# Batch 0's chain with 4 zero products instead of 43, reordered slots, a fill on GpSimd, and the last two blocks as one more pair

## The chip, the cores and the metric

One NeuronCore of one Trainium2 chip. The metric is the device time of one execution in microseconds (us); every number of a run is the median of its fast executions unless said otherwise. A run is called slow when it is over 1.5% above the fastest of the same kernel. Engine names as the profile has them: PE is TensorE's products, PEld its weight loads, DVE VectorE, ACT ScalarE, POOL GpSimd, SP SyncE; a q behind the name is that engine's issue of transfers.

## The reference, cut to what matters

```python
# B = 8 batches, H = 8 heads, S = 576, D = 64, M = 32 memories, d_model = 512, d_ff = 1536
a = softmax over s of phi                 # bhsm
k_m, v_m = a.T @ k, a.T @ v               # bhmd
attn = softmax(q @ k_m.T / 8) @ v_m       # bhsd
x = attn as 4608 tokens x 512
out = ((x @ w_a) * (x @ w_b)) @ w_out     # float32 in and out
```

The kernel never builds `attn`. It multiplies the 32 memories of each head into `w_a` and `w_b` (a "fold", result `vab`), so that the up products are `A` (the normalised scores, 256 rows) times `vab`. The down products of two blocks of 128 tokens are done together with seven half-size products instead of eight (a "pair", with sums of tokens and of weights made ahead on GpSimd).

## The kernel before: the parts that the change touches

The program is written by units that are placed by hand into slots between the up products; the strings below are that schedule. `f3` is three zero products (they keep TensorE busy), `y3` three early down products, `ks`/`vs` the sums of k and v, `kt`/`vt` their transposes, `s`/`e`/`den`/`nr` scores, exp, denominators and the normalising product that gives `A`, `hv`/`v` a fold of 256 or 512 columns and `hx`/`x` its copy to SBUF. "Second weights" below means `w_b`; a transfer's "landing" is the time at which its data have arrived.

```python
    nc.vector.memset(kv_sbs[1][:, 2], 1.0 / CS)      # ones beside k and v of odd batches
    load_wab(256, 512)
    load_wab(512, 1024)
    load_wab(1024, 1536)
    load_wo(0); load_phi(1); load_k(1); load_q(1, halves[0]); load_wo(1); ...   # cut
    load_wo(2)

        def normalise(g, hfs=slice(0, 2)):
            ...                                       # R = exp(-L) on ScalarE
            engine = nc.vector if b < 3 else nc.gpsimd
            engine.tensor_tensor(out=attn[b][:, g, sl], in0=t["E"][:, g, sl], in1=t["R", g][:, sl], op=ALU.mult)

    def sum_weights():                                # four GpSimd sums of w_out's quarters
        ...
            nc.gpsimd.tensor_tensor(out=out, in0=in0, in1=in1, op=ALU.subtract)

    fill(16)
    chain(0, "exp0 exp1 ks0 f3 kt0 qt0 qt1 f14 s0 e0 ks1 f3 kt1 qt2 qt3 f6 den0 f4 s1 nr0 e1 f6 vs0 vs1 vt0 vt1 den1 f3 "
             "hv0a hx0a nr10 nr11 hv0b hx0b f4")
    ups(steps(0, 0, 4), slots(0, "- hv1a+hx1a - hv1b+hx1b - v1a+x1a - v1b+x1b"))
    load(2)
    ups(steps(0, 4, 12), slots(0, "- - - - v2a+x2a - v2b+x2b"))
    chain(1, "exp0 exp1 y9 ks0 y3 kt0 qt0 qt1 y1 ks1 y3 kt1 s0 e0 qt2 qt3 y6 den0 y2 s1 e1 nr0 y4 den1 y2 vs0 vs1 y1 vt0 vt1 nr1 y1 hv0a hx0a y2 hv0b hx0b y2")
    load(3)
    sum_weights()
    ups(steps(1, 0, 4), slots(1, "y1 hv1a+hx1a hv1b+hx1b y1 v1a+x1a v1b+x1b y3 y3"))
    ...                                               # batches 2 to 7, cut
    last_down(B // 2 * NI - 1)                        # last block: 12 + 12 products of 256 columns
```

The softmax here doesn't subtract the row's maximum and nothing guards it: scores larger than these inputs give would overflow.

## Time and profile before

| | before |
|---|---|
| time, 3 runs | 247.96 us (247.90 to 247.97) |
| span of the profiled run | 246.4 us |
| TensorE busy | 234.4 us (95%) |
| first up product | 20.45 us |
| last fold of batch 0's second weights | 31.45 us |
| batch 1's first early down product (its load) | 36.09 us |
| first single-half up step of batch 1 | 57.08 us |
| last up product done (first load of the rest) | 228.70 us |
| last weight load done | 241.86 us |
| last store's issue starts | 243.29 us |

The page's part 4, the chain that ended last by engine, says that transfers hold a sixth of it (all of them ahead of 48.4 us):

```profile
PE 74%; DMA 17%; DVE 3%; POOL 2%; ACT 1%; issue 1%; ACTq 0%; DVEq 0%; POOLq 0%
```

### The profile page before, as it was taken

How to read it: one execution, taken by the hardware profiler on the slowest of the kernel's cores; microseconds unless marked ns; L12 is line 12 of the kernel's file. 1: busy time of each engine (PE TensorE's matmuls, PEld its weight loads, DVE VectorE, ACT ScalarE, POOL GpSimd, SP SyncE). 2: the span in 40 equal slices, each digit the busy share in tenths (PEclk: the TensorE clock that was granted, in tenths of full speed). 3: DMA queues.
4: the chain of work that ended last, by engine and by line, in shares of the span. 5: the costliest groups of instructions: out<-in, count | busy, mean ns of one | idle time of the engine just before them, and what ended most of it. 6: DMA issues, size and time to landing. Idle time of an engine off the chain costs nothing.

```text
span 246.4 us, 7681 instructions
## 1 busy us (share of the span) xinstructions
PE 234.4 (95%) x3049; PEld 167.1 (68%) x3049; DVE 166.5 (68%) x401; ACT 157.9 (64%) x409; POOL 151.1 (61%) x123
## 2 busy tenths in 40 slices
PE   7589999999998999999999999999999999999993
PEld 3354574456655857777787777877787787888782
DVE  3636794477959967876994649865995686756620
ACT  2247772578697489578856768588855877565330
POOL 8724233499799029892899759892849186936000
PEclk9999999999999999999999999999999999999999
DMA  6999999999979804973159732695120303033145
GB/s 198 210 198 206 211 252 207 255 220 271 233 183 207 160 4 108 238 127 85 33 149 208 174 85 45 167 207 145 32 56 3 88 7 82 10 78 71 43 104 128
DMA packets 26036, 33.82 MB, mean 137 GB/s; under 512 B 1936, under 2 KB 20368, under 8 KB 26000
## 3 DMA queue, kind: packets, MB, share of 16 engines
q0 software_dynamic: 19280, 22.71, 50.3%
q1 hardware_dynamic: 6288, 9.90, 16.3%
q10 hardware_dynamic: 432, 0.72, 0.8%
q8 instruction: 24, 0.39, 0.6%
q14 instruction: 12, 0.10, 0.1%
HBM read 42.47 MB, written 9.44 MB: 211 GB/s over the span
## 4 chain that ended last, share of the span: by engine, by line
PE 74%; DMA 17%; DVE 3%; POOL 2%; ACT 1%; issue 1%; ACTq 0%; DVEq 0%; POOLq 0%
PE pa L602 18%; PE pb L612 16%; PE py L480 15%; PE pv L480 8%; DMA phi_sb<-in_phi_dram 6%; DMA wo_sb<-in_moe_w_out_dram 6%; DMA wb_sb<-in_moe_w_b_dram 5%; PE pva L337 5%; PE px L480 4%; PE po L389 3%; PE pkv L213 2%; PE pD L314 1%; PE pscore L292 1%; PE pT L242 1%; POOL q_sb L90 1%
## 5 line engine op out<-in xcount | busy, mean ns | idle before, releaser
L615 DVE TENSOR_TENSOR ht<-a_sb,pb 128x288 f16<-128x288 f16 x192 | 82.9, 448 | 40.2 <-ACT a_sb L605 29.3
L605 ACT CAST a_sb<-pa 128x288 f16<-128x288 f32 x192 | 74.7, 405 | 31.6 <-PE pa L602 31.0
L602 PE MATMUL pa<-A,vab 128*128 128x288 f16 x384 | 76.5, 287 | 1.4 <-DVE A L325 1.4
L612 PE MATMUL pb<-A,vab 128*128 128x288 f16 x384 | 76.5, 286 | 0.2
L463 POOL TENSOR_TENSOR h_sums<-ht 128x768 f16<-128x768 f16 x28 | 45.9, 1640 | 34.0 <-DVE ht L615 34.0
L612 PEld LDWEIGHTS <-vab 128*128 128x128 f16 x384 | 37.0, 98 | 13.2 <-issue 1.9
L602 PEld LDWEIGHTS <-vab 128*128 128x128 f16 x384 | 34.5, 98 | 15.9 <-issue 9.1
L480 PEld LDWEIGHTS <-h_sums 128*128 128x128 f16 x360 | 35.1, 98 | 6.5 <-issue 0.4
L349 ACT CAST vab<-pva 128x512 f16<-128x512 f32 (+1 forms) x52 | 28.1, 558 | 10.0 <-PE pva L337 10.0
L349 DVE CAST vab<-pva 128x512 f16<-128x512 f32 (+1 forms) x52 | 32.8, 643 | 2.4 <-PE pva L337 2.0
L480 PEld LDWEIGHTS <-ht 128*128 128x128 f16 x270 | 26.4, 98 | 5.4 <-issue 0.2
L480 PE MATMUL py<-w_sums,h_sums 128*128 128x256 f16 x180 | 28.5, 272 | 0.0
L463 POOL TENSOR_TENSOR h_sums<-h_sums,ht 128x768 f16<-128x768 f16 x14 | 23.1, 1650 | 1.0
L463 POOL TENSOR_TENSOR h_sums<-ht,h_sums 128x768 f16<-128x768 f16 x14 | 23.0, 1642 | 1.0
L305 ACT ACTIVATE E<-pscore 128x288 f16<-128x288 f32 x32 | 11.4, 416 | 13.6 <-PE pscore L292 13.5
L325 POOL TENSOR_TENSOR A<-E,R 128x576 f16<-128x576 f16 x10 | 12.8, 1278 | 11.9 <-ACT R L323 11.6
L389 PE MATMUL po<-wo_sb,ht 128*128 128x512 f16 x60 | 16.0, 381 | 0.1
L480 PE MATMUL py<-wo_sb,ht 128*128 128x256 f16 x90 | 15.2, 273 | 0.0
L480 PE MATMUL pv<-w_sums,h_sums 128*128 128x256 f16 x90 | 15.2, 273 | 0.0
L204 DVE STREAM_TRANSPOSE qT<-q_sb 128x288 f32<-128x288 f32 x32 | 14.5, 463 | 0.6 <-DMA q_sb<-in_q_dram 0.6
L480 PE MATMUL py<-w_sums,ht 128*128 128x256 f16 x90 | 14.7, 272 | 0.1
L315 ACT ACTIVATE L<-pD 128x288 f32<-128x288 f32 x32 | 11.4, 413 | 5.0 <-PE pD L314 4.8
(66 smaller groups left out, 273.1 us busy)
## 6 DMA issues: line engine op xcount, KB each, us to landing
out_dram<-o_sb SPq DMA_DIRECT2D x70, 128.0 KB, 2.4
kv_sb<-in_v_dram POOLq DMA_DIRECT2D x7, 576.0 KB, 10.5
phi_sb<-in_phi_dram POOLq DMA_DIRECT2D x7, 576.0 KB, 4.6
kv_sb<-in_k_dram POOLq DMA_DIRECT2D x7, 576.0 KB, 8.2
q_sb<-in_q_dram POOLq DMA_DIRECT2D x6, 576.0 KB, 12.8
wo_sb<-in_moe_w_out_dram POOLq DMA_DIRECT2D x3, 512.0 KB, 17.4
q_sb<-in_q_dram POOLq DMA_DIRECT2D x4, 288.0 KB, 12.7
wa_sb<-in_moe_w_a_dram POOLq DMA_DIRECT2D x2, 512.0 KB, 14.8
```

Of the source, the lines that this page charges most:

```text
L204: nc.vector.transpose(out=t["qT"][:, hp, :].bitcast(F32), in_=qs[b][:, hp, :].bitcast(F32))
L305: nc.scalar.activation(out=Ev[:, g, :, z, :], in_=pss, func=AF.Exp, scale=1.0 / (8.0 * CS))
L325: engine.tensor_tensor(out=attn[b][:, g, sl], in0=t["E"][:, g, sl], in1=t["R", g][:, sl], op=ALU.mult)
L337: nc.tensor.matmul(t["pva", lo, z][g][0][32 * j:32 * j + 32, 0:hi - lo], t["kvT"][64 * r:64 * r + 64, 4 + g, M * j:M * j + M], w_sbs[z][64 ...
L349: engine_copy(out=vabs[b][z][:, g, lo:hi], in_=pva[:, 0:hi - lo])
L389: nc.tensor.matmul(po, ht[:, i, P * c:P * (c + 1)], wo_sb[:, i, :], start=(i == 0), stop=(i == NFF - 1))
L463: engine.tensor_tensor(out=out, in0=in0, in1=in1, op=op)
L480: nc.tensor.matmul(po, lhs[:, i], rhs[:, i], start=first and i == 0, stop=i == KH - 1, skip_group_check=not first)
L602: nc.tensor.matmul(pa, vab[0][:, g, fs], A[:, g, HALF * hf:HALF * (hf + 1)], start=(g == 0), stop=(g == 1))
L605: nc.scalar.copy(out=a_sb, in_=pa)
L612: nc.tensor.matmul(pb, vab[1][:, g, fs], A[:, g, HALF * hf:HALF * (hf + 1)], start=(g == 0), stop=(g == 1))
L615: nc.vector.tensor_tensor(out=ht[:, i, t0:t0 + HALF], in0=a_sbs[hf - hfs[0]], in1=pb, op=ALU.mult)
```

## The change

Its intent: shorten batch 0's chain of small steps (which runs with most engines idle), take a fill of ones off VectorE, place the slots of the later batches anew, and do the last two blocks as one more pair. The core of the diff:

```diff
-    nc.vector.memset(kv_sbs[1][:, 2], 1.0 / CS)
     load_wab(256, 512)
...
     load_wo(2)
+    nc.gpsimd.memset(kv_sbs[1][:, 2], 1.0 / CS)
...
-    PAIRED = range(EARLY + PLAIN, BLOCKS - 2, 2)
+    PAIRED = range(EARLY, BLOCKS, 2)
...                                    # in two_downs, ends = the last pair
         plus(o2[:, NH:], y, u5)
+        if ends:
+            store(o2, cidx + 1, slice(NH, d_model))
...
-        store(o2, cidx + 1)
+        if ends:
+            store(o2, cidx + 1, slice(0, NH), (nc.sync, nc.scalar))
+        else:
+            store(o2, cidx + 1)
...                                    # sums of the last two pairs on VectorE instead of the last one
-            yield from down(BLOCKS - 2)
...
-    chain(0, "exp0 exp1 ks0 f3 kt0 qt0 qt1 f14 s0 e0 ks1 f3 kt1 qt2 qt3 f6 den0 f4 s1 nr0 e1 f6 vs0 vs1 vt0 vt1 den1 f3 "
-             "hv0a hx0a nr10 nr11 hv0b hx0b f4")
-    ups(steps(0, 0, 4), slots(0, "- hv1a+hx1a - hv1b+hx1b - v1a+x1a - v1b+x1b"))
+    chain(0, "exp0 exp1 ks0 kt0 qt0 qt1 f2 s0 e0 ks1 kt1 den0 qt2 qt3 f2 s1 nr0 e1 vs0 vs1 den1 vt0 vt1 nr10 nr11 hv0a hx0a")
+    ups(steps(0, 0, 4), slots(0, "hv0b+hx0b hv1a+hx1a - hv1b+hx1b - v1a+x1a - v1b+x1b"))
...
-    ups(steps(0, 4, 12), slots(0, "- - - - v2a+x2a - v2b+x2b"))
-    chain(1, "... y1 ks1 y3 kt1 s0 e0 qt2 qt3 y6 den0 y2 s1 e1 nr0 y4 den1 y2 vs0 vs1 y1 vt0 vt1 nr1 y1 hv0a hx0a y2 hv0b hx0b y2")
+    ups(steps(0, 4, 12), slots(0, "- - - - v2a+x2a+v2b+x2b - -"))
+    chain(1, "... y1 y3 ks1 qt2 s0 e0 y6 kt1 qt3 den0 y3 s1 nr0 e1 y4 y2 den1 vs0 vs1 vt0 y1 vt1 nr1 hv0a hx0a hv0b y3 hx0b y2")
...                                    # slots of batches 1 to 7, cut
-    last_down(B // 2 * NI - 1)
```

More of the change, by code (lines that the diff above doesn't have):

```diff
@@ L404, in down @@
         yield from down_part(po, bank, cidx, 0, NFF)
-    def last_down(cidx):
-        pair, c = divmod(cidx, NI)
-        w = d_model // 2
-        for x in range(2):
-            cs = slice(w * x, w * (x + 1))
-            po = banks.tile([P, w], F32, name="pl")
-            o_sb = opool.tile([P, w], F32, name="o_sb")
-            for i in range(NFF):
-                nc.tensor.matmul(po, ht[:, i, P * c:P * (c + 1)], wo_sb[:, i, cs],
-                                 start=(i == 0), stop=(i == NFF - 1))
-            nc.scalar.mul(out=o_sb[:, :w // 2], in_=po[:, :w // 2], mul=1.0 / (CS * CS))
-            nc.vector.tensor_scalar(out=o_sb[:, w // 2:], in0=po[:, w // 2:], scalar1=1.0 / (CS * CS), scalar2=None,
-                                    op0=ALU.mult)
-            for z, engine in enumerate((nc.sync, nc.scalar)):
-                slot = 2 * c + z
-                engine.dma_start(out=out_rows[2 * pair + slot // NI, slot % NI, :, cs],
-                                 in_=o_sb[64 * z:64 * z + 64, :])
     EARLY = 4
@@ L464, in sum_tokens, with store @@
             yield
-    def store(o_sb, cidx):
+    def store(o_sb, cidx, cs=slice(0, d_model), engines=(nc.sync, nc.sync)):
         pair, c = divmod(cidx, NI)
@@ L469, in store @@
             slot = 2 * c + z
-            nc.sync.dma_start(out=out_rows[2 * pair + slot // NI, slot % NI], in_=o_sb[64 * z:64 * z + 64, :])
+            engines[z].dma_start(out=out_rows[2 * pair + slot // NI, slot % NI, :, cs], in_=o_sb[64 * z:64 * z + 64, cs])
     def two_downs(self, cidx):
@@ L476, in two_downs @@
         scale = 1.0 / (CS * CS)
+        ends = cidx == PAIRED[-1]
         def products(po, lhs, rhs, first=False):
@@ L529 @@
     LEAD = 24
-    PLAIN = 0
-    PAIRED = range(EARLY + PLAIN, BLOCKS - 2, 2)
+    PAIRED = range(EARLY, BLOCKS, 2)
     class Work:
@@ L544, in products @@
         def products(self):
-            for cidx in range(EARLY, EARLY + PLAIN):
-                yield from down(cidx)
-            for cidx in PAIRED[:-1]:
+            for cidx in PAIRED:
                 yield from two_downs(self, cidx)
-            yield from down(BLOCKS - 2)
-            yield from two_downs(self, PAIRED[-1])
         def add_up(self):
@@ L554, in add_up @@
                 for x in range(4):
-                    yield n, NFF * PLAIN + 7 * KH * n + KH * (x + 1)
+                    yield n, 7 * KH * n + KH * (x + 1)
                     if x == 0:
-                        sums = sum_tokens(cidx, nc.gpsimd if n < len(PAIRED) - 1 else nc.vector)
+                        sums = sum_tokens(cidx, nc.gpsimd if n < len(PAIRED) - 2 else nc.vector)
                     next(sums)
@@ L586, in plan @@
             self.summed = n
-            self.ready = NFF * min(PLAIN, tokens // P - EARLY) + 7 * KH * n + NFF * (tokens // P >= BLOCKS - 1)
+            self.ready = 7 * KH * n
             self.rate = max(0, self.ready - self.done - keep) / slots
@@ L686 @@
-    chain(1, "exp0 exp1 y9 ks0 y3 kt0 qt0 qt1 y1 ks1 y3 kt1 s0 e0 qt2 qt3 y6 den0 y2 s1 e1 nr0 y4 den1 y2 vs0 vs1 y1 vt0 vt1 nr1 y1 hv0a hx0a y2 hv0b hx0b y2")
+    ups(steps(0, 4, 12), slots(0, "- - - - v2a+x2a+v2b+x2b - -"))
+    chain(1, "exp0 exp1 y9 ks0 y3 kt0 qt0 qt1 y1 y3 ks1 qt2 s0 e0 y6 kt1 qt3 den0 y3 s1 nr0 e1 y4 y2 den1 vs0 vs1 vt0 y1 vt1 nr1 hv0a hx0a hv0b y3 hx0b y2")
     load(3)
     sum_weights()
-    ups(steps(1, 0, 4), slots(1, "y1 hv1a+hx1a hv1b+hx1b y1 v1a+x1a v1b+x1b y3 y3"))
@@ L690 @@
-    ups(half_steps(1, 0, 4), slots(1, "- v2a+x2a+v2b+x2b+qt0' - exp0' - exp1'+qt1' - qt2'+kv'+km'+y9"))
+    ups(steps(1, 0, 4), slots(1, "- hv1a+hx1a hv1b+hx1b+y1 - v1a+x1a y3+v1b x1b y3"))
+    ups(half_steps(1, 0, 4), slots(1, "- v2a+x2a+v2b+x2b+qt0' - - qt1'+exp0'+qt2' exp1' - kv'+km'+y9"))
     work.plan(S + HALF, 10)
-    ups(half_steps(1, 1, 4), slots(2, "qt3 kvt - sc+e0+e1+den0 - nr0+den1+v0+x0a - - x0b+nr1 - v1+x1b+x1a -"))
-    second = "v2_+x2a_+exp0 x2b_ - exp1 qt0+kv+km - qt1+kvt+qt2 qt3 sc+e0 - e1+v0+x0a x0b den0+v1+x1a nr0+L x1b+exp0' den1 - nr1+v2+x2a - x2b+exp1' qt0' kv'+qt1' km' - qt2'+kvt'+qt3'"
@@ L694 @@
-    every = "- sc+e0 e1 den0 v0+x0a+x0b - - nr0 exp0' - v1+x1a x1b+qt0' den1 - exp1' v2+x2a+x2b nr1+qt1' - kv'+km' qt2' kvt'+qt3' L - -"
-    last = "sc+e0 - e1 - v0 x0b den1+x0a - den0 - nr0+v1+x1a nr1 x1b - - - - - - v2+x2a - - - x2b"
+    ups(half_steps(1, 1, 4), slots(2, "- kvt qt3 sc+e0+e1+den0 - nr0+den1+v0+x0a - - x0b+nr1 - v1+x1b x1a"))
+    second = "v2_+x2a_+exp0 x2b_ exp1 - qt0+kv+km - qt1+qt2 kvt+qt3 sc+e0 - e1+v0+x0a den0+x0b v1+x1a nr0+L x1b+exp0' den1 - nr1+v2+x2a - x2b+exp1' - qt0'+kv'+qt1' km' - qt2'+kvt'+qt3'"
@@ L696 @@
+    every = "- sc+e0 e1 den0 v0+x0a+x0b - - nr0+exp0' - - v1+x1a qt0' x1b+den1 exp1' - v2+x2a+x2b nr1+qt1' kv'+km' qt2' - qt3' - kvt'+L -"
+    last = "sc+e0 - e1 - v0+x0b - x0a den1 - - den0 v1+x1b x1a+nr0 - - - - nr1+v2+x2a - - - - - x2b"
     for b in range(2, B):
```

## The prediction

> **What bounds the kernel now.** I read the page first, then the chain that ended last, then the order-of-time view for 0 to 52 us, for 62 to 78 us and from 224 us on, because the change touches those three stretches.
>
> From the page (shares of the span; busy tenths in 40 slices of 6.2 us; DMA is the share of 16 engines):
>
> ```profile
> PE 234.4 (95%) x3049; PEld 167.1 (68%) x3049; DVE 166.5 (68%) x401; ACT 157.9 (64%) x409; POOL 151.1 (61%) x123
> ...
> PE   7589999999998999999999999999999999999993
> ...
> DMA  6999999999979804973159732695120303033145
> ```
>
> TensorE is the bound from slice 4 on. In slices 2 to 13 the DMA engines are full as well, so the front has two limits. The chain of waits (start, length, what) shows which of them counts there:
>
> ```profile
> 5.69 12.22 DMA wb_sb<-in_moe_w_b_dram
> 17.91 0.28 issue
> 18.19 15.25 DMA phi_sb<-in_phi_dram
> 33.44 14.95 DMA wo_sb<-in_moe_w_out_dram
> 48.38 0.04 issue
> 48.43 0.59 PE po L389 x2
> ```
>
> Up to 48.4 us this is a chain of transfers. The built program says why: GpSimd's transfers use eight semaphores in turn, so the ninth issue waits until the first has landed. Adding each issue's "to landing" time to its start gives: first quarter of the second weights (wb) 17.9 us, its second quarter 9.09 + 11.3 = 20.4, middle thirds of wa and wb 9.81 + 13.1 = 22.9 and 10.55 + 14.9 = 25.5, last thirds 11.57 + 16.4 = 28.0 and 14.38 + 16.2 = 30.6, phi of batch 1 18.19 + 16.4 = 34.6, k of batch 1 37.3, last third of w_out 48.4. No compute instruction sets these; they depend on the order of issue alone.
>
> From the order of time (start, length; in brackets the idle time before and its releaser), batch 0's chain:
>
> ```profile
> 8.04 1.98 DVE L165 MEMSET kv_sb<- 128x2304 f16 x1 [0.43 <-issue]
> ...
> 9.94 0.10 DVE L265 RECIPROCAL rphi<-pk 128x1 f32<-128x1 f32 x1
> ...
> 10.64 1.70 PE L151 MATMUL pw<-warm 128*128 128x256 f16 x14
> ...
> 21.14 0.61 PE L602 MATMUL pa<-A,vab 128*128 128x288 f16 x3 [0.38 <-DVE A L325]
> ...
> 30.36 0.66 PE L612 MATMUL pb<-A,vab 128*128 128x288 f16 x4
> ...
> 31.45 0.41 PE L337 MATMUL pva<-wb_sb,kvT 64*32 64x512 f16 x8
> ```
>
> The first sums of k are done at 8.5 us, but the reciprocal that uses them waits behind a fill of ones until 9.94. Later 14 zero products stand ahead of the scores. The last fold of the second weights (31.45) comes 0.85 us after its weights land.
>
> The end:
>
> ```profile
> 239.25 2.61 PEld L415 LDWEIGHTS <-ht 128*128 128x128 f16 x24
> ...
> 242.23 0.28 ACT L417 ACTIVATE o_sb<-pl 128x128 f32<-128x128 f32 x1 [1.03 <-PE pl L415]
> 242.54 0.29 DVE L418 TENSOR_SCALAR o_sb<-pl 128x128 f32<-128x128 f32 x1 [1.01 <-ACT o_sb L417]
> 242.64 1.19 SPq L422 DMA_DIRECT2D out_dram<-o_sb  x2
> ```
>
> **What the Trainium skill says.** "TensorE: Matmul & The Clock Gate", Part 1, sections "What's actually happening" and "Wait — 56ns, not 53.3ns?": the array runs at half clock until a window of about 3.4 us has been busy, and drops again after an idle one; warm, a product of N columns takes N/2.4 ns plus about 2.5 ns. The trace agrees on the pace: 24 loads of the last block in 2.61 us are 109 ns each (256 columns: 109.2), 12 plain products of 512 columns in 2.59 us of the chain are 216 ns. It agrees on the start too: ten of the first 16 zero products go at 0.43 us, the last six at 0.2. Whether the thinner chain stays warm no run of the kernel before shows. "SBUF — State Buffer", section "SBUF: two separate sides": VectorE and GpSimd share a port pair that is locked for a whole instruction when VectorE reads two SBUF inputs and GpSimd reads SBUF. The trace agrees: the product that makes A takes 0.46 us alone and 1.42 us beside a GpSimd sum (below). "DMA: Bandwidth & Descriptors", section "Issuing engines are not separate DMA queues": all queues end on the same 16 engines; so a leaner compute chain cannot speed a full DMA row. The row of nines agrees.
>
> **The change, part by part.**
>
> *Batch 0's chain.* The fill of ones (1.98 us) leaves VectorE, so the reciprocal can go at 8.6 instead of 9.94: 1.35 us. Thirty-nine of 43 zero products go (39 x 0.109 = 4.3 us of TensorE busy time, mostly in waits). The 14 held the scores back from 11.8 (transposes done) to 12.28: 0.5 us. Second denominators right after the sums of v, and the fold of the second weights moved behind the first up products, take off more. Stepping through with the durations of the trace (sums 0.7, copy 0.3, two transposes 0.83, exp 0.7, A 0.46) I get scores at 10.6, denominators at 12.5, sums of v from 14.2, the first up product at about 17 instead of 20.45 (its rest 21.14). That is 3 to 4 us gained, locally.
>
> *Where that gain ends.* The first second-weight fold now waits for 17.9 us. The middle folds, 25.2 and 26.64 before, come to stand at 22.9 and 25.5, which are landings. After that five half-steps of 0.49 us and a short wait for a cast bring TensorE to the last folds at about 28.4; wa has landed (28.0), wb not until 30.6. So TensorE idles some 1.9 us. The change also issues both last folds together, before the second products of step 6. Before, at 30.36 us, those products ran first. After: fold at 30.6, products at 30.97; before: products at 30.36 and the same 0.34 us fold later. Net 30.97 - 30.36 - 0.34 = 0.27 us *later* when batch 1's chain starts, 36.35 against 36.09. The whole front gain is lost to the transfer of the weights. Batch 1's chain then meets the last third of w_out at 48.4 us, as before; it gets there with its second fold done and leaves with 37 early down products done instead of 36. Front in sum: -0.2 us (one product of 0.216), give or take 0.4.
>
> *The ones on GpSimd.* The fill stands after the last w_out issue (33.44 + 0.76 = 34.2). From a 128-element fill (0.22 us) and a 1-element one (0.10 us) I estimate 0.12/127 x 2304 + 0.1 = 2.3 us, so done at 36.5; the sums of batch 1 need it at 38.2. The next issue (phi of batch 2) moves from 35.1 to 36.6 and is needed at 60 us. Zero.
>
> *The middle.* Batches 1 to 7 get the same instructions in other slots. Two clear stalls of TensorE stand there:
>
> ```profile
> 68.24 0.41 PE L314 MATMUL pD<-E,ones 128*128 128x288 f16 x2 [0.57 <-ACT E L305]
> ...
> 73.70 1.42 DVE L325 TENSOR_TENSOR A<-E,R 128x576 f16<-128x576 f16 x1
> ...
> 75.17 0.28 PE L602 MATMUL pa<-A,vab 128*128 128x288 f16 x1 [1.01 <-DVE A L325]
> ```
>
> Scores, exp and denominators stay in one slot, so the 0.57 stays. The second stall depends on whether a GpSimd sum stands beside A; slots around it move, so it may shrink by up to 1 us or stay. All idle time of TensorE after 50 us is some 2.1 us (busy times by stretch). I take -0.3, with -1.2 to +0.7 possible.
>
> *The end.* Two plain blocks (12 products of 512 and 24 of 256: 2.59 + 2.62 = 5.21 us) become one more pair of 42 products of 256: 42 x 0.109 = 4.59. That is -0.62 us on TensorE's path. The last eviction was ScalarE 0.28 and then VectorE 0.29 in a row (242.23 to 242.83); now one ScalarE pass of 0.38: -0.2. But SyncE must issue two half stores, two full ones and one more after it, at about 0.57 us each, from about 240.5: its last starts near 242.75 against 243.25. So the end gains 0.5, not 0.8. The sums of the last two pairs now are VectorE's; the first of them runs at about 230.5, is ready at 231.1 and is needed at 232.0: no wait.
>
> Sum: -0.2 - 0.3 - 0.5 = -1.0 us: 247.96 - 1.0 = 246.9 us.
>
> **Rivals.** (1) *The front gain survives*: then 243.5 to 245. For it: the chain loses 3 us of waits that are plain in the trace. Against it: the landings above, and the full DMA row. It needs wb earlier than 30.6, and nothing in the issue order is changed before that. (2) *TensorE goes cold* in the thin chain: between 8 and 17 us only about half of the time is busy. Cold up products take 0.24 us instead of 0.12, so a cold spell of 3.4 to 7 us could add 2 to 3 us before 28 us. For it: the author of the kernel had put 43 fills there. Against it: there are 4 us of waiting for weights to absorb it. Only if it lasts beyond 30 us does it count: 247.5 to 249. (3) *New stalls in the middle*: a moved copy or transpose that ends last. For it: copies of several halves are pushed a slot later; against it: VectorE and ScalarE are 55 to 88% busy in the 10 us stretches there, with some room. 248 to 249.
>
> **Range and chances.** The parts spread by about 0.4 (front), 0.9 (middle), 0.4 (end), so about 1.1 together; with the rivals, 245.5 to 248.3 holds it 8 times in 10. Two per cent is 4.96 us. TensorE's removable time after 48.4 us is 0.2 + 2.1 + 0.8 = 3.1 us, so faster by over 2% needs rival 1 in full: 3%. Slower by as much has no source but a long cold spell: 1%.
>
> **What would show it.** In the changed profile: the reciprocal near 8.6 us; first up products near 17 to 18.5; waits for wb before folds, the longest ending near 30.6; batch 1's first early product near 36.3; a landing of w_out at 48.4 on the chain; some 5 us less busy time of TensorE with nearly the same span; 42 products of 256 columns at the end, 0.109 us each. I am wrong if the weights land clearly earlier than 30.6, if up products stand at 0.24 us each after 30 us, if the sums of batch 1 wait for the fill on GpSimd, or if a stall over 1 us appears after 50 us.

## The result, and the profile after

The changed kernel takes 247.91 us (247.85 to 248.02, 4 runs) against 247.97 of the kernel before in the same rounds: ratio 0.9997, 95% interval 0.9979 to 1.0014. (A ratio compares fast runs of the same rounds, so it is not quite the ratio of the medians quoted.) Two more groups on other chips, below, gave 0.9984 and 0.9990; over the three the change is worth some 0.1%, about 0.25 us, and each of the three intervals takes in no change at all. I had forecast 1.0 us.

| | before | after | predicted after |
|---|---|---|---|
| span of the profiled run | 246.4 us | 246.2 us | |
| TensorE busy | 234.4 us | 233.1 us | some 5 us less |
| first up product | 20.45 | 18.24 | 17 to 18.5 |
| last fold of batch 0's second weights | 31.45 | 30.66 | 30.6 |
| batch 1's first early down product | 36.09 | 36.28 | 36.3 |
| first single-half up step of batch 1 | 57.08 | 57.01 | -0.2 against before |
| last up product done | 228.70 | 228.36 | -0.5 against before |
| last weight load done | 241.86 | 241.15 | |
| last store's issue starts | 243.29 | 243.08 | 242.75 |

The page after: the granted clock is no longer 9 throughout, and the chain of waits is no longer one of transfers.

```profile
PEclk9855999999999999999999999999999999999999
...
PE 89%; DVE 3%; DMA 3%; ACT 2%; issue 1%; DVEq 0%
```

Slices 3 and 4 (12 to 25 us) stand at 5: half clock. In the order of time after (start, length; the idle time before and its releaser in brackets), the same places as in the prediction's view of before:

```profile
8.48 0.17 DVE L265 RECIPROCAL rphi<-pk 128x1 f32<-128x1 f32 x1 [0.94 <-PE pk L256]
...
18.24 1.14 PE L584 MATMUL pa<-A,vab 128*128 128x288 f16 x4 [0.49 <-ACT vab L349]
...
29.52 0.65 PE L584 MATMUL pa<-A,vab 128*128 128x288 f16 x4
...
30.66 0.11 PEld L337 LDWEIGHTS <-kvT 64*32 64x32 f16 x8 [0.45 <-DMA wb_sb<-in_moe_w_b_dram]
...
31.00 0.66 PE L594 MATMUL pb<-A,vab 128*128 128x288 f16 x4
...
34.26 2.04 POOL L177 MEMSET kv_sb<- 128x2304 f16 x1
```

The reciprocal stands at 8.48 instead of 9.94. Four up products take 1.14 us at 18.24 and 0.65 at 29.52: the same work at half and at full clock. The last fold's weight load waits for `w_b` (0.45 us), and batch 1's chain starts at 36.28 against 36.09 (a difference that single profiles don't resolve, see below). GpSimd's fill is done at 36.3, in time for the sums at 38.4.

One more place matters for the reading, the first of the four wide folds, before and after:

```profile
25.21 0.41 PE L337 MATMUL pva<-wa_sb,kvT 64*32 64x512 f16 x8
```

```profile
25.29 0.41 PE L337 MATMUL pva<-wa_sb,kvT 64*32 64x512 f16 x8
```

The 2.2 us that the changed kernel was ahead at the first up product are gone here, 5 us before the last weights land: in this profile the half clock took them.

The end after:

```profile
235.95 1.19 PEld L462 LDWEIGHTS <-ht 128*128 128x128 f16 x11 [0.21 <-issue]
237.15 2.67 PEld L462 LDWEIGHTS <-h_sums 128*128 128x128 f16 x24
...
241.47 0.38 ACT L508 ACTIVATE o_sb<-py 128x256 f32<-128x256 f32 x1 [2.23 <-PE py L462]
```

and, asked from 240.6 us on, SyncE's issues (five in a row):

```profile
240.59 3.03 SPq L451 DMA_DIRECT2D out_dram<-o_sb  x5
```

The last eviction ends at 241.85, 0.98 us sooner than before (242.83). But the last of SyncE's five issues starts only at 243.08, 0.21 us sooner than before: the span moved by 0.2.

### The profile page after: what moved, and what is told of

It reads as the page before. It is cut to its first block, busy times and chain, and to the rows that moved or that the text cites. A ratio compares the mean times of both kernels' runs of the same rounds, so it can differ in the third digit from the quotient of the medians.

```text
span 246.2 us, 7624 instructions
## 1 busy us (share of the span) xinstructions
PE 233.1 (95%) x3016; PEld 165.7 (67%) x3016; DVE 168.6 (68%) x405; ACT 158.6 (64%) x410; POOL 152.8 (62%) x124
## 4 chain that ended last, share of the span: by engine, by line
PE 89%; DVE 3%; DMA 3%; ACT 2%; issue 1%; DVEq 0%
PE pa L584 21%; PE pb L594 19%; PE py L462 16%; PE pv L462 8%; PE pva L337 6%; PE po L389 5%; PE px L462 4%; DMA phi_sb<-in_phi_dram 3%; PE pkv L213 2%; PE pD L314 2%; PE pscore L292 2%; PE pk L256 2%; PE pT L274 1%; PE pT L242 1%; ACT a_sb L587 1%
## 5 line engine op out<-in xcount | busy, mean ns | idle before, releaser
L584 PE MATMUL pa<-A,vab 128*128 128x288 f16 x384 | 77.4, 291 | 1.6 <-DVE A L325 1.1
L594 PEld LDWEIGHTS <-vab 128*128 128x128 f16 x384 | 37.5, 99 | 13.4 <-issue 1.7
L584 PEld LDWEIGHTS <-vab 128*128 128x128 f16 x384 | 34.9, 99 | 16.1 <-issue 8.7
L462 PEld LDWEIGHTS <-h_sums 128*128 128x128 f16 x384 | 37.4, 98 | 6.9 <-issue 0.4
L462 PEld LDWEIGHTS <-ht 128*128 128x128 f16 x288 | 28.1, 98 | 5.6 <-issue 0.4
L462 PE MATMUL py<-w_sums,h_sums 128*128 128x256 f16 x192 | 30.3, 272 | 0.0
L462 PE MATMUL py<-wo_sb,ht 128*128 128x256 f16 x96 | 16.0, 273 | 0.0
L462 PE MATMUL pv<-w_sums,h_sums 128*128 128x256 f16 x96 | 16.0, 272 | 0.0
L469 ACT ACTIVATE u<-py 128x256 f32<-128x256 f32 x32 | 12.4, 387 | 5.2 <-PE py L462 5.0
L462 PE MATMUL py<-w_sums,ht 128*128 128x256 f16 x96 | 15.5, 272 | 0.1
L462 PE MATMUL px<-wo_sb,ht 128*128 128x256 f16 x96 | 15.4, 273 | 0.0
```

Source lines behind the costliest of these rows:

```text
L462: nc.tensor.matmul(po, lhs[:, i], rhs[:, i], start=first and i == 0, stop=i == KH - 1, skip_group_check=not first)
L469: nc.scalar.mul(out=x, in_=po, mul=scale)
L584: nc.tensor.matmul(pa, vab[0][:, g, fs], A[:, g, HALF * hf:HALF * (hf + 1)], start=(g == 0), stop=(g == 1))
L594: nc.tensor.matmul(pb, vab[1][:, g, fs], A[:, g, HALF * hf:HALF * (hf + 1)], start=(g == 0), stop=(g == 1))
```

## The experiments

Fifteen runs in four groups; each group shares its runs of the kernel before. Different executions of the same front code differ too: the kernel with only the end changed has its first early down product at 35.82 us where the kernel before has 36.09, with the same instructions up to there. Single profiles are therefore read for the length of a stretch, and differences of starts under 0.3 us are not read at all.

### Front and end alone

`end_only`: the changed kernel with the kernel before's schedule strings and its fill on VectorE.

> The kernel before with only the end changed: the last two plain blocks become one more pair, the last eviction one ScalarE pass, the last sums on VectorE. My theory after reading both traces: the pair costs TensorE 4.8 us (loads at 0.111 us, one wait of 0.2 us for a bank) against 5.1 for the two plain blocks, so TensorE ends about 0.3 to 0.4 us earlier, but SyncE has five stores to issue in a row from about 241 us at 0.6 us each, so its last one still starts at about 243.2: time 247.9 to 248.1, no gain over before. Rival (my prediction's step): the end is worth 0.5 us, time 247.4 to 247.5. A second rival, that the end costs time and the rest gains it: over 248.3.

Measured: 248.22 us against 248.07, ratio 1.0004 (0.9979 to 1.0030). From the last up product to the last weight load 12.80 us, as in the changed kernel (12.79) and against 13.16 in the kernel before; the last store's issue starts 1.6 us after the last eviction's start. From that up product to the end of the span it is 17.88 us, as in the changed kernel, and 17.57 to 17.74 in the three profiles with the old end. The end by itself is worth nothing, as the theory had it, and not the 0.5 us of my prediction.

`front_only`: the kernel before with batch 0's chain, the up steps beside it and the fill changed.

> The kernel before with only batch 0's chain, the up products beside it and the fill of ones on GpSimd changed. Theory: the chain runs at half clock from about 10 to 24 us and then waits for the last third of the second weights at 30.6 us; batch 1's first early product starts at 36.3 to 36.5 against 36.1, and the wait for w_out at 48.4 us takes that up: time 247.9 to 248.3. Rival: some of the 3 us gained in the chain comes through, time under 247.3.

Measured: 247.71 us against 248.07, ratio 0.9977 (0.9954 to 0.9999). My theory had 247.9 or more, the rival under 247.3: it fell between, a gain of about 0.4 us by the medians and 0.6 by the ratio, which the interval barely parts from none. Its clock dropped less (0.72 to 0.84 between 10 and 25 us), so the wait for the weights is plainer there: second of the last two folds, order of time,

```profile
30.38 0.11 PEld L337 LDWEIGHTS <-kvT 64*32 64x32 f16 x8 [1.33 <-DMA wb_sb<-in_moe_w_b_dram]
```

and batch 1's first early product at 36.01.

The changed kernel's other two profiles (`after_again` and `after_third`, below) say the same. The first was at half clock only from 19.5 to 22.9 us; its wide folds did come forward (24.10), and then TensorE waited for the last third of `w_b`:

```profile
30.51 0.41 PE L337 MATMUL pva<-wb_sb,kvT 64*32 64x512 f16 x8 [1.19 <-DMA wb_sb<-in_moe_w_b_dram]
```

Its first early product came at 36.13; in `after_third` (half clock from 17.4 to 24.3 us) that fold stands at 30.29 and the product at 35.91. So whatever the half clock leaves of the gain, the landing takes.

### The half clock and the weights

`warm`: the changed kernel with 31 zero products in batch 0's chain.

```diff
-    chain(0, "exp0 exp1 ks0 kt0 qt0 qt1 f2 s0 e0 ks1 kt1 den0 qt2 qt3 f2 s1 nr0 e1 vs0 vs1 den1 vt0 vt1 nr10 nr11 hv0a hx0a")
+    chain(0, "exp0 exp1 ks0 f3 kt0 qt0 qt1 f5 s0 e0 ks1 f3 kt1 f3 den0 qt2 qt3 f5 s1 nr0 f3 e1 vs0 vs1 f2 den1 vt0 f3 vt1 nr10 nr11 hv0a hx0a f4")
```

> The changed kernel with 31 zero products in the waits of batch 0's chain instead of 4, so that TensorE stays at full clock. Theory: the clock row shows 9 throughout, the up products of 18 to 24 us cost 0.12 us each instead of 0.24, and none of it reaches the end, because the last fold of the second weights starts at 30.6 to 30.8 either way and batch 1's first early product at 36.3 to 36.5: time 247.8 to 248.0. Rival: the half clock costs 0.5 us or more, time under 247.5.

Measured: the six runs were 247.55, 248.18, 248.46, 248.79, 251.78 and 252.22 us; ratio of the fast ones 0.9997 (0.9969 to 1.0025). In the profile the clock was still down to 0.85 and 0.81 from 15 to 25 us, so the run tests little of what it was made for; the last fold again waited for the weights, at 30.12. The two slow runs were not expected by either theory; no profile of them was kept.

To take the weights' landing away, three kernels load only a quarter of the rows of the last two thirds of `w_a` and `w_b`, and VectorE zeroes the rest while it is idle (result wrong, all products still run):

```diff
+        c = slice(0, NHP) if lo < 512 else slice(0, 1)
-        nc.gpsimd.dma_start(out=wa_sb[:, :, lo:hi], in_=wa_rows[:, :, lo:hi])
+        nc.gpsimd.dma_start(out=wa_sb[:, c, lo:hi], in_=wa_rows[:, c, lo:hi])      # and wb alike
+    for lo in (512, 1024):
+        for w_sb in (wa_sb, wb_sb):
+            nc.vector.memset(w_sb[:, 1:, lo:lo + 512], 0.0)
```

`light_before`:

> The kernel before, but of the last two thirds of both first weights only a quarter of the rows is loaded and the rest set to zero on VectorE while it has nothing else to do (the result is wrong on purpose; every product still runs). All later landings come some 7 us earlier. Both theories: this kernel never waited for those weights, only 0.15 us for w_out at 48.4 us, so it stays within 0.4 us of before: 247.5 to 248.1.

Measured: 247.99 us against 247.94; first early down product of batch 1 at 35.82. As expected, nothing.

`light_after`:

> The changed kernel with the same three quarters of those weights left out. Theory (the landing of the second weights at 30.6 us takes the gain of the chain, the half clock takes what the landing leaves): the last folds now start one behind the other, batch 1's first early product 0.2 to 1.5 us earlier than the 36.3 of the changed kernel, no wait for w_out; time 0.3 to 1.3 us below the light form of before: 246.4 to 247.5. Rival (the weights are not what binds; the half clock alone takes it): nothing earlier than 36.1, time within 0.2 us of the light form of before.

Measured: 250.76 us, ratio 1.0103 (1.0074 to 1.0132): *slower* by 2.5 us. Both theories failed on the time. The first early product stands at 35.59, 0.23 us ahead of the light form of before, the lower edge of what I expected. The loss comes later:

`light_warm`:

> The light form of the changed kernel with 31 zero products in the chain. If the clock stays full and no weights bind, batch 1's first early product should stand 1 to 2 us before the 36.1 of before and the time at 246.0 to 247.2. If it equals the light form without the zero products, the half clock was not the remaining limit but the pace of casts and products is. The same kernel with all weights had the clock at 0.81 to 0.85 from 15 to 25 us, after a 1.37 us pause at the 223rd product, so I expect part of it only: 0.2 to 0.8 us below the light changed kernel.

Measured: 251.06 us (six runs from 249.53 to 252.16). With the clock at 9 up to 50 us and no weights to wait for, the first early product stands at 34.62, 1.2 us ahead of the light form of before: so the landing and the half clock together had been taking the front's gain, and either is nearly enough (without the landing but at half clock 0.23 us are left; at full clock but with the landing, in `old_chain1` below, none). And again more than 3 us are lost right after.

### What the light kernels ran into

All three profiles with such a loss (the two light forms with the new chain of batch 1, and a slow run of the changed kernel with spread stores) show one event: the second normalising product `A` of batch 1. Order of time, first the light form of before:

```profile
47.59 0.45 DVE L329 TENSOR_TENSOR A<-E,R 128x576 f16<-128x576 f16 x1
```

the light form of the changed kernel:

```profile
47.75 4.24 DVE L329 TENSOR_TENSOR A<-E,R 128x576 f16<-128x576 f16 x1
```

and the slow run with spread stores, with GpSimd and TensorE around it:

```profile
48.66 0.74 POOL L85 DMA_DIRECT2D kv_sb<-in_v_dram  x1 [3.40 <-PE pT L274]
49.33 4.24 DVE L325 TENSOR_TENSOR A<-E,R 128x576 f16<-128x576 f16 x1
49.39 0.75 POOL L90 DMA_DIRECT2D q_sb<-in_q_dram  x1
50.14 3.10 POOL L429 TENSOR_TENSOR w_sums<-wo_sb 128x1536 f16<-128x1536 f16 x1
53.33 3.18 POOL L429 TENSOR_TENSOR w_sums<-wo_sb,w_sums 128x1536 f16<-128x1536 f16 x1
...
53.97 0.90 PE L584 MATMUL pa<-A,vab 128*128 128x288 f16 x3 [2.78 <-DVE vab L349]
```

VectorE's product ends at 53.57, just after GpSimd's first sum of weights (50.14 + 3.10 = 53.24), although it started 0.81 us before that sum. TensorE waits 2.78 us for the copies behind it and comes out at half clock (three products in 0.90 us). In each of the three cases GpSimd's two issues and its sum stand back to back, and `A` starts 0.05 or 0.06 us before the second issue. Back to back alone is not enough: they stand so in the light form of before, too, but there `A` starts 0.22 us before the second issue and takes 0.45 us (the same in `light_warm_old1` and `best`). The change moved `A` there: the second denominators come after `y4 y2`, and `A` starts at 48.44 in the changed kernel instead of 47.85. In that profile, of a fast run, the q issue happens to wait until 48.80, and `A` is through at 48.89.

`light_warm_old1`: the light warm kernel with batch 1's chain string of the kernel before, nothing else.

> The light form (three quarters of the last two thirds of the first weights left out, result wrong on purpose) of the changed kernel with the 31 zero products in batch 0's chain, and with batch 1's chain as the kernel before has it. The same kernel with the new batch 1 chain took 251.06 us: its second product A (4.24 us instead of 0.45) stood beside GpSimd's weight sums. Theory: with the old chain that product comes 1 us earlier against GpSimd's issues and takes 0.45 us; the 1.2 us gained at the first early product (34.6 against 35.8 in the light form of before) then come through: 246.2 to 247.2. Rival: the product is slow whatever the chain's order, because GpSimd's weight sums start earlier with the light load: 250 to 251.5.

Measured: 247.05 us (five of six runs 246.75 to 247.19, the sixth 249.35, of which no profile was kept), against 251.06 with the new string:

```profile
46.39 0.45 DVE L329 TENSOR_TENSOR A<-E,R 128x576 f16<-128x576 f16 x1
```

The theory holds: the order of that chain makes the slow mode of the light kernels, and without it most of the 1.2 us of the front reaches the last up product (227.17 us, against 228.25 in the light form of before) and the end.

`old_chain1`: the changed kernel with the old string for batch 1.

```diff
-    chain(1, "... y4 y2 den1 vs0 vs1 vt0 y1 vt1 nr1 hv0a hx0a hv0b y3 hx0b y2")
+    chain(1, "... y4 den1 y2 vs0 vs1 y1 vt0 vt1 nr1 y1 hv0a hx0a y2 hv0b hx0b y2")
```

> The changed kernel with batch 1's chain as before, the rest as changed. Theory: no run in the slow mode of 251 to 254 us (the changed kernel had one in six on the last chip), because the product A ends before GpSimd's issues stand back to back; fast runs as the changed kernel's or up to 0.3 us faster: 247.4 to 247.9. Rival: the slow runs are the chip's and not the order's; then they come here too.

Measured: 248.35 us (248.27 to 248.86), ratio 1.0006 (0.9984 to 1.0027). No slow run in six, as expected, though that says little where the changed kernel has one in 15; and the fast time is above my 247.9. Here the clock stayed at full, and TensorE waited 1.1 and 1.4 us for two parts of `w_b`; the first early product came at 36.36. The excess lies later. From the first single-half up step to the last up product the traces of all kernels agree within 0.03 us for the same strings: 171.62 us with the old slots (4 profiles), 171.34 with the new ones (10), but 172.08 in `old_chain1`, `mix` and `light_warm_old1`. These three join the old string of batch 1 to the new slots, and the two don't fit: together they call one early down product fewer than either kernel does, so five instead of four are left for the slot at 63 us, and TensorE loses 0.74 us between 57 and 65 us (0.22 of it is that product; what makes the rest I did not trace). Some 0.25 us of that was saved ahead of that step (the product that moved). So this kernel doesn't show what the old order costs or gains by itself.

`after_again`, the changed kernel once more:

> The changed kernel itself, unchanged, so that the other runs of this group have it on the same chip. Within 0.3% of before again (247.3 to 248.6). One more thing to look for: in the slow run of the kernel with spread stores the product A of batch 1 took 4.24 us beside GpSimd's weight sums; if the changed kernel stands near that collision, one or two of its runs will be 3 to 5 us slow.

Measured: 247.80 us against 247.94, ratio 0.9984 (0.9964 to 1.0004), with one run of 253.51 among five of 247.73 to 247.85. The profile is of a fast run, so that this one run is the collision is likely, not shown. Among the changed kernel's 15 runs it is the only one; the kernel before had none above 249.61 in 48.

### The stores of the last pair

`spread_stores`:

```diff
-            store(o2, cidx + 1, slice(NH, d_model))
+            store(o2, cidx + 1, slice(NH, d_model), (nc.sync, nc.scalar))
-        store(o1, cidx)
+        store(o1, cidx, engines=(nc.sync, nc.gpsimd) if ends else (nc.sync, nc.sync))
```

> The changed kernel with the last pair's stores spread: of the early half stores one goes to ScalarE's queue, of the full ones one to GpSimd's; nothing else. Theory: SyncE's queue of five stores sets the end; with three left on it the last one starts at about 241.9 instead of 243.1, so the time falls by 0.6 to 1.1 us to 246.8 to 247.3. Rival: the end is set by TensorE and the transfers' own 2 us, the queue is not the limit, time within 0.15 us of the changed kernel. GpSimd's store may land late (software descriptors); then the gain is smaller, 0.2 to 0.5.

Measured: 247.74 us, ratio 0.9971 (0.9948 to 0.9994), one run of 253.10 (the profiled one, shown above). About 0.3 us (by the ratio 0.7) below before, and only the lowest of its five fast runs (247.06) lies in the range expected; the group has no run of the changed kernel to compare with.

`one_store`: only the first line of that edit, so that one of the early half stores goes to ScalarE's queue.

> The changed kernel with one store moved: of the two early half stores of the last pair, one goes to ScalarE's queue, which is idle there. Theory (SyncE's row of five stores sets the end): four are left, the last starts about 0.6 us sooner after ScalarE's last eviction (1.0 instead of 1.6 us after that eviction starts), and the stretch from that start to the end of the span shrinks from 4.7 us to 4.1 to 4.3; time 0.4 to 0.6 us below the changed kernel of the same group. Rival (the transfers' own 2 us and the closing steps set it): stretch and time unchanged within 0.15.

Measured: 247.49 us, ratio 0.9975 (0.9963 to 0.9987), against 247.71 of the changed kernel in the same rounds. SyncE's issues end 0.6 us sooner after the last eviction's start:

```profile
241.34 0.38 ACT L508 ACTIVATE o_sb<-py 128x256 f32<-128x256 f32 x1 [2.23 <-PE py L462]
```

and, asked from 242.4 us on, SyncE's last issue:

```profile
242.32 0.55 SPq L451 DMA_DIRECT2D out_dram<-o_sb  x1
```

0.98 us after it, against 1.61 in the changed kernel. The stretch from that eviction to the end of the span shrank from 4.76 to 4.45 us, not to the 4.1 to 4.3 expected: the queue is part of the limit, and something of 0.3 us behind it I did not find. The runs of the two kernels overlap (247.19 to 247.70 against 247.55 to 248.04), so the size of the gain is rough.

`after_third`, beside it:

> The changed kernel again, for the same chip as its neighbours: fast runs 247.6 to 248.0, span from the last eviction's start to the end 4.7 us, perhaps one slow run of 251 to 254.

Measured: 247.71 us (247.55 to 248.04), ratio 0.9990 (0.9976 to 1.0004); 4.76 us from eviction to end; no slow run in five.

### Versions that take all of it together

`mix`: old chain of batch 1, last fold back in its old slot, spread stores.

> The changed kernel with the old chain of batch 1, the last fold of the second weights put back behind the products of step 6 and the first of step 7, and the last pair's stores spread over three queues. Sum of my terms: 0.27 us for the fold, 0.5 to 0.7 for the stores, against 247.9: 246.9 to 247.3. Rival (the stores gain nothing because the transfers land together anyway): 247.5 to 247.8.

Measured: 248.14 us, ratio 0.9991 (0.9971 to 1.0011). A miss. The first early product came at 34.82, 1.3 us sooner than before, as the fold no longer blocked the products, but then TensorE waited 0.4 us for k of batch 1 and 0.5 for `w_out`, both transfers, and the first up product of batch 1 was loaded at 49.16 against 49.41 before: 0.25 us were left. A further part went in the misfit of old string and new slots: the middle took 172.09 us here and 171.63 in the kernel before.

`mix_early`: that, with the 31 zero products and the last four early down products moved behind the first up products of batch 1.

> As the one above, with the 31 zero products in batch 0's chain and the last early down products of batch 1's chain moved behind the first up products, so that neither the half clock, nor the last fold, nor w_out's last third at 48.4 us is waited for. If those three are the front's limits, batch 1's first early product stands at 35.0 to 35.7 and the time is 0.4 to 0.8 us below the one above: 246.2 to 246.8. Rival: other landings (k and v of batch 1 at 37.3 and 45.7) take it up: equal to the one above within 0.2.

Measured: 247.31 us against 248.06, ratio 0.9963 (0.9943 to 0.9983), 0.8 us below `mix` but above what I expected. Its front was not early at all (first early product at 35.94: a pause of 2.1 us in batch 0's sums, for which the profile has no releaser). Its strings fit together again, and its middle takes 171.33 us instead of 172.09; against `mix` its last up product stands 0.22 us sooner, and the stretch from there to the end is 0.36 us shorter.

`best`: the same with one store on ScalarE in place of the one on GpSimd.

> The changed kernel with the 31 zero products in batch 0's chain, the last fold put back, batch 1's old chain with its last four early down products moved behind the first up products, and one store moved to ScalarE. With the same front and a GpSimd store besides, 247.31 was measured against 248.06 of before. Expected 246.9 to 247.4, no slow run of 251 or more, and at least 0.4 us below the changed kernel of this group. Rival: the gain of that run was the chip's, then it is within 0.2 us of the changed kernel.

Measured: six runs of 247.19, 247.24, 247.36, 248.83, 248.93 and 250.98 us; ratio of the fast ones 0.9994 (0.9968 to 1.0020). It has two modes. The profiled run (248.93) is a bad one: clock at 0.5 in slice 4 in spite of the zero products, first early product at 37.16. The run of 250.98, without a profile, also shows that the old order of batch 1 doesn't rule out slow runs. It doesn't beat the others dependably, and so the 247.31 us of `mix_early`, nearly the same program, are not to be counted on either. What was measured beside both kernels and is below both is the one moved store: 247.49 us.

## Why the prediction was right or wrong

**The mechanism of the front was right, its sizes were not.** The chain gained (reciprocal 8.48, first up product 18.24 instead of 20.45), and the gain ended at the landing of the last third of `w_b`: that fold stands between 30.29 and 30.66 in the three profiles of the changed kernel, where I had 30.6, and batch 1 at 35.91 to 36.28, where I had 36.35. The way there was another one in the profile shown. I had the wide folds come forward to landings at 22.9 and 25.5 and 1.9 us of idle time before the last fold; they stood at 25.29 and 26.72, as in the kernel before, and 0.45 us was waited: the half clock had used the rest. Rival 2 named that cold spell and said that the wait for the weights would absorb it; it did, though the spell lasted some 14 us (10.8 to 24.4) instead of 3.4 to 7. That it ate just about the slack, and no more, is luck; `after_again`, with a short spell, waited 1.19 us instead. `light_warm_old1` shows the other half: without that landing and with the clock kept, about 1 us comes through. Two signs that I had named failed: TensorE's busy time fell by 1.3 us and not by 5, as the products at half clock took longer (1.14 us for four instead of 0.65), and the landing of `w_out` is not on the chain that ended last.

**The middle was right in size**: -0.3 predicted; from 57.01/57.08 to the last up product the changed kernel gains 0.27, and all ten profiles with its later slots agree (171.34 us against 171.62 in the four with the old ones). What in the slots does it wasn't tested, so the size may be luck: I had allowed -1.2 to +0.7. The stall of 1 us before batch 2's first products stayed, with `A` at 1.48 us beside a GpSimd sum.

**The end failed**, in the step "SyncE must issue two half stores, two full ones and one more after it, at about 0.57 us each, from about 240.5: its last starts near 242.75 ... So the end gains 0.5, not 0.8".

| term of the end | predicted | measured |
|---|---|---|
| TensorE: pair for two plain blocks | -0.62 | -0.37 (13.16 to 12.79 us) |
| last eviction | -0.2 | -0.27 (0.97 to 0.70 us from last load to eviction done) |
| SyncE's row of stores | +0.3 | +0.77 (data ready 0.98 sooner, issued 0.21 sooner) |
| sum | -0.5 | +0.13 |

I took 0.109 us for each of the pair's 42 products; 24 loads took 2.67 us, 0.111 each, and a wait of 0.21 us came with it (the weight loads pause with "issue" just where a bank is written again that VectorE reads between two sums for the next pair; that the sums cause it is argued, not shown). Larger is the queue. I had its start at 240.5 without moving it by the 0.5 us that I credited to front and middle, so the term could not be right if the rest was; measured, it starts at 240.59, each issue takes 0.61 us on average, and the last store leaves 1.23 us after its data are ready (before: 0.46). `end_only` (ratio 1.0004) and `one_store` (0.6 us off the queue, 0.22 us off the time) agree: the end gave nothing, because stores that leave one after the other took back what TensorE and the eviction gave. Together -0.07 - 0.27 - 0.37 - 0.27 + 0.77 = -0.21 us, the change of the span; the term of the front was -0.2 in the prediction and is below what single profiles resolve.

**What I did not see** is that the new order of batch 1 moves `A` next to GpSimd's issues and sums of weights. I checked that lock for batch 2 only, where the trace before already showed it. In the profiles of fast runs it costs nothing; in the light kernels it turned a gain of up to 1.2 us into a loss of 2.5 to 3.

**Open**: what the remaining 0.3 us of the stretch behind the last eviction are; whether the pause in batch 0's chain is the fetch of instructions that stands before it (last section); why 0.22 us ahead of GpSimd's issue is enough for `A` and 0.05 is not; and whether the slow runs without a profile (`after_again`, `warm`, `best`) are the collision.

## What to carry to other kernels

A gain in a chain is worth no more than the time to the next landing: list the landings from issue and "to landing", and step the new chain against them before counting. When work at the end gets shorter, follow the last results through the queue that stores them; five issues of 0.6 us in a row can take back all that TensorE gave. And when an order is changed, look at what a VectorE product with two SBUF inputs comes to stand beside on GpSimd: here 0.05 us or 0.22 us ahead of a GpSimd issue went with 4.24 us or 0.45 us. And before a string of one version is joined to the slots of another, count what both call: one product too few went with 0.5 us of loss in `old_chain1`.

## What the Trainium skill lacked or had wrong

- "SBUF — State Buffer", "SBUF: two separate sides": it says that of a VectorE operation with two SBUF inputs and a GpSimd operation that reads SBUF, whichever starts first has the shared ports. Here VectorE's product started 0.81 us before GpSimd's sum, 0.05 or 0.06 us before a transfer issue on GpSimd, and still ended only after that sum (4.24 us instead of 0.45, three profiles; the profile's spans on GpSimd are rough). No run here separates the part of the issue from that of the sum behind it.
- "TensorE: Matmul & The Clock Gate", Part 1: its table gives an idle window of about 3.4 us as what drops the clock (a later section of that Part tells of many short idles that do it too, without saying how many). Here the clock was at half from 10.8 to 24.4 us, though TensorE's longest pause after the first zero products was 1.54 us and it was busy 2.50 of the 5 us from 5 to 10 us; and the chain with 31 zero products was cold for a while in two profiles (`warm`, `best`) and not in three others.
- "DMA: Bandwidth & Descriptors", "Issuing engines are not separate DMA queues": it calls the sequencer's time for an issue usually small beside the transfer. For these 64 to 128 KB stores an issue took 0.47 to 0.60 us (0.51 to 0.70 from one start to the next) against 1.9 to 2.5 us to landing, and five in a row are part of what sets the end of the kernel.
- "Runtime: NRT & Kernel Launch", "Instruction fetch mechanics": it calls the cost of fetching the next 16 KiB of a program mostly hidden. TensorE pauses with nothing named as releaser right after the 223rd product of the program, wherever that falls in the chain: 0.76 us (before), 1.37 (`warm`), 2.09 (`mix_early`), 0.93 (`old_chain1`); only in the first profile of the changed kernel is it as short as 0.11. In each of the 17 profiles one 16 KB packet of the kind "instruction" lands 1.3 to 1.6 us before the 224th product starts (before: 16.54 and 18.06 us; `mix_early`: 15.80 and 17.33). That the fetch is the cause is argued from this, not shown: no run moved it.
- "GPSIMD Engine Reference", "Common operations" names memset without a cost: 2304 f16 elements took 2.04 us on GpSimd and 1.98 on VectorE.
